# Case: the first W' tile from unsplit float32 pieces, stores issued by ScalarE, and earlier slots for w_out and w1/w2

## The chip, the cores and the metric

The kernel runs on one core of one Trainium2 chip. The metric is the time of one execution in microseconds on the device. Each engine works through its own list of instructions in order and waits for others through semaphores: PE (TensorE, matrix products), DVE (VectorE), ACT (ScalarE), POOL (GpSimd) and SP (SyncE, which here only issues DMAs).

## The reference

Three blocks follow each other, all in float32: attention with a decay by the running sum of `log f`, then two feed-forward blocks on the 2304 tokens of width 512.

```python
scores = scale * q @ k.T + cum[:, None] - cum[None, :]      # 4 x 8 heads, 576 x 576, causal
x = softmax(scores) @ v                                     # 2304 x 512
h = x @ w_in;  g = h * tanh(softplus(h));  x = g @ w_out    # 512 -> 2048 -> 512
h = (x @ w1) * (x @ w2) @ w3;  y = h @ w_out2               # 512 -> 1024 -> 1024 -> 512
```

## The kernel before

**Precision.** PE multiplies in a reduced float32 form ("fp32r" in the rows) at a high pace, so a product that must keep float32 accuracy is made of three: each operand is split into a rounded half `hi` and a rest `lo`, and hi·hi, hi·lo and lo·hi are added in PSUM (`MM_PAIRS`). A split is a cast by ACT (L98) and a subtraction by DVE (L102) or, in two pieces of 256 columns, by POOL (L112). Scores from raw q and k, the transposes and P·V use plain float32 operands.

**Weights.** The host passes them as 64-bit words. A piece of 128 x 512 is loaded (512 KB, L122) and converted by one ACT instruction (L133, `cv_exp`) and three DVE instructions (L141 to L143, `cv_bits`).

**Two phases.** Phase A (to about 380 us) works through 16 pairs of heads, four *sub-slots* (slots in the code) a pair, 64 in all and a few behind them. In a slot stand score products, softmax (minimum on DVE, L391; exponential on ACT, L401), transposes on PE (L438) with their copies out of PSUM by ACT and DVE (L453), and in every fourth slot P·V. Between them `run_filler` puts products of weights:

- Slots 0 to 20: W' = w3 @ w_out2, in eight tiles of 24 products (`wp_unit`, L521). Tile f needs two pieces of w3 (`t{f}0`, `t{f}1`) and all eight of w_out2 (`o0` to `o7`). The order of the tiles is `FS`: 0, 4, 1, 5 and so on. The ten pieces of the first tile are loaded, converted and split ahead of slot 0, with the subtractions on DVE (`lo_eng`); those of the later tiles are prepared in the slots, with POOL subtracting.
- From slot 21: the first layer x @ w_in (`l1_unit`, L552), 24 products a slot to slot 36, then 12. Each unit of 12 products is copied to a tile `h` (three buffers, L556) and stored to `h_scr` (L557).

Beside these, `job` gives pieces their slots: loading, conversion and what follows one slot later. w_out's pieces (`u`) start at `W_OUT_SLOT`; from pairs of them POOL forms sums and `build` (L837 to L850) writes seven split tiles a pair to DRAM through five rotating buffers (`pt`, `bs`). Four pieces of w1 and w2 (`v`) are converted and stored at slots 56 to 62. Phase B (from about 385 us) runs the feed-forward layers.

**Order.** PE's order is written out by hand. The other engines' orders come from a list scheduler that runs when the kernel is built; ahead of slot 0, ACT's, DVE's and SP's are by hand too. All DMAs are issued by SP. A DMA counts up one of eight semaphores in turn (`DMAHW0` to `DMAHW7` in the orders), and one that takes a semaphore again first waits for the DMA that had it eight DMAs before, unless another wait covers that.

`plan` (L589) spreads the 192 products of W' over slots 0 to 20 in the shares 26, 24, 22 and 24 of a pair's four slots. `R` (L420) is a pair's row of inverse sums, loaded from `inv_scr`, where `inv_rows` stored it; P·V's result is multiplied by it (L483).

Of the kernel before, what the change touches and what calls it, by code (L numbers as in the profile page):

```python
# [24 lines left out]
TB = S // 2  # L25
# [21 lines left out]
W_IN_SLOT = 16  # L47
L1_BOTH = 6
W_IN_STEP = 0.8
W_OUT_SLOT = 30  # L50
W_OUT_STEP = 1.8
V_SOON = 4
L1_S = (21, 37)
SHARE = (26, 24, 22, 24)

# [20 lines left out]
class Kernel:  # L76
# [48 lines left out]
    def cv_exp(self, key):  # L125
        raw = self.cv[key][0]
        if key in self.soon:
            t = self.x_tile(f"cv{key}", F32)[:, :512]
        else:
            t = self.att.tile([128, 512], F32, name=f"cv{key}", tag="cv", bufs=CV)  # L130
        self.cv[key][1] = t
        hw = raw.rearrange("p (n w) -> p n w", w=2)[:, :, 1]
        self.nc.scalar.activation(t, f32(hw), AF.Copy, scale=F64_EXP)  # L133

    def cv_bits(self, key):

# [275 lines left out]
    def inv_rows(self, p):  # L412

        nc = self.nc
        t = self.att.tile([16, 128], F32, name=f"inv{p}", tag="inv", bufs=1)
        with self.tc.high_priority(offset=HP_SM):
            nc.scalar.copy(t[0:9], self.ps_t[1][0:9, 384:512])
        nc.sync.dma_start(self.inv_scr[p], t[0:9])

    def inv_load(self, p):  # L420
        self.R = self.att.tile([128, S], F32, name=f"R{p}", tag="R", bufs=1)
# [80 lines left out]
    def w3_split(self, f, k):  # L502
# [2 lines left out]
        hi, lo = self.w3s[f]  # L505
        self.cv_split(f"t{f}{k}", hi[:, 512 * k:512 * k + 512], lo[:, 512 * k:512 * k + 512])

    def wp_unit(self, f):

        mm = self.nc.tensor.matmul  # L510
        steps = []
        box = []

        def step(g, k, i):
            if i == 0:
                box.append(self.l1_bank())
            o = box[0]
            a, b = MM_PAIRS[k]
            w = self.w3s[f][a][:, 128 * g:128 * g + 128]
            x = self.wo2t[g][:, 512 * b:512 * b + 512]  # L520
            mm(o, w, x, start=i == 0, stop=i == 23)  # L521
            if i == 23:
                t = self.w_tile(0, f"wp{f}", F32)[:, :512]
                with self.tc.high_priority(offset=HP_L1):
                    self.nc.scalar.copy(t, o)
                self.nc.sync.dma_start(self.wp_scr[f], t)

        i = 0
        for g in range(8):
            for k in range(3):  # L530
                steps.append(((f"t{f}{g // 4}", f"o{g}"), lambda g=g, k=k, i=i: step(g, k, i)))
                i += 1
        return steps
# [6 lines left out]
    def l1_unit(self, b, m, half):  # L540
        mm = self.nc.tensor.matmul
        steps = []
        box = []

        def step(c, k, i):
            if i == 0:
                box.append(self.l1_bank())
            o = box[0]
            a, bb = MM_PAIRS[k]
            w = self.wi[m][:, 512 * a + 128 * c:512 * a + 128 * c + 128]  # L550
            x = self.X[4 * b + c, half][:, TB * bb:TB * bb + TB]
            mm(o[:, :TB], w, x, start=i == 0, stop=i == 11)  # L552
            if i == 11:
                t = self.base.tile([128, TB], F32, name=f"h{b}_{m}_{half}", tag="h", bufs=HB)
                with self.tc.high_priority(offset=HP_L1):
                    self.nc.scalar.copy(t, o[:, :TB])  # L556
                self.nc.sync.dma_start(self.h_scr[128 * m:128 * m + 128, b * S + TB * half:b * S + TB * half + TB], t)  # L557

        i = 0
        for c in range(4):  # L560
            for k in range(3):
                steps.append(((f"i{m}",), lambda c=c, k=k, i=i: step(c, k, i)))
                i += 1
        return steps
# [23 lines left out]

    def plan(self):  # L589

        cnt, acc, done = [], 0.0, 0
        share = [SHARE[s % NU] for s in range(WP_END)]
        for x in share:
            acc += 192 * x / sum(share)
            k = min(192, int(acc + 0.5)) - done
            cnt.append(k)
            done += k
        cnt += [24] * (L1_S[1] - WP_END) + [12] * 22 + [0] * (NU * NPAIR - L1_S[1] - 22)
# [2 lines left out]
    def phase_a(self):  # L601
# [5 lines left out]

        first = []
        for q in range(2):
            first.append((f"t0{q}", self.cols(self.w3t, 0, q), self.w3_split, 0, q))  # L610
            for g in range(4 * q, 4 * q + 4):
                first.append((f"o{g}", self.rows(self.wo2, g), self.wo2_split, g))
        where = [None, None, 8, 8, 8, 8, 0, 0, 0, 0]
        def early(a, z):
            for i in range(a, z):
                self.cv_load(first[i][0], first[i][1], where[i])

        def go(i):
            self.cv_exp(first[i][0])
            self.last = self.cv_bits(first[i][0])  # L620

        def fin(i):
            first[i][2](*first[i][3:])

        self.consts()
        self.lo_eng = "dve"
        with self.tc.manual_schedule(engines={getattr(mybir.EngineType, e) for e in ("Activation", "DVE", "SP")}):
# [6 lines left out]
            for i in range(1, len(first)):  # L634
                go(i)
                if i == HOLD:
                    self.hold = self.last
                fin(i - 1)
            fin(9)
        self.lo_eng = "pool"  # L640
        self.go_act, self.go_sp = self.last_act, self.last_sp

# [7 lines left out]
        def job(s, key, src, fin, *a, lag=1):  # L650
            at(max(0, s - 1), self.cv_load, key, src)
            conv.setdefault(s + lag, []).append(key)
            at(s + lag + 1, fin, *a)

        jobs = [(f"t{f}{q}", self.cols(self.w3t, f, q), self.w3_split, f, q) for f in FS[1:] for q in range(2)]
        for i, j in enumerate(jobs):
            job(int(W3_STEP * i), *j)
# [9 lines left out]
                for k in range(2):  # L667
                    at(s + 4 + k, self.build, 0, u, k)
        for f in range(V_SOON):
            job(NU * NPAIR - 8 + 2 * f, f"v{f}", self.v_src(f), self.cv_store, f"v{f}", self.w12_scr[f])  # L670
        at(32, self.x_places, 1)
        for p in range(4, 8):
            for half, s in ((0, (32, 33, 34, 36)), (1, (38, 38, 39, 40))):
# [8 lines left out]
                for hh in range(2):  # L682
                    at(s + 1, self.load_cum, 2 * p + 2 + hh)

        for f in FS:
            self.filler.extend(self.wp_unit(f))
        self.S, self.nsm, self.act, self.dve = {}, 0, None, None
        with self.tc.manual_schedule(engines={mybir.EngineType.PE}):
# [647 lines left out]
```

## Time and profile before

| | |
|---|---|
| median of 3 runs | 930.57 us (929.39 to 933.74) |
| profiled execution | 932.73 us, span 930.8 us |
| PE busy | 876.7 us, 94% of the span |
| DVE, ACT, POOL busy | 688.4, 499.0, 147.4 us |
| DMA queue of SP | 189.0 MB, 63.7% of 16 engines' span |

The profiled execution lies 2.2 us above the median, and 1.9 us of it lie around the span. A matmul's busy time is modelled and overlaps the next; two starts in a row give the pace. Durations below are of this execution.

### The profile page before, as it was taken

The numbers are of one execution on the slowest core, as the hardware profiler recorded it, in microseconds if no ns is written. First come the engines' busy times: TensorE is split into PE (matmuls) and PEld (weight loads), VectorE is DVE, ScalarE is ACT, GpSimd is POOL, SyncE is SP. The second block draws the span as 40 slices with busy tenths as digits, with TensorE's granted clock in tenths as the row PEclk, the third lists the DMA queues.
The fourth block names the chain that finished last, engine by engine and source line by source line (L and its number), as shares of the span: only waits on it lengthen the run. The fifth ranks groups of instructions, "written<-read, shape, count | busy, mean of one in ns | idle before, by whom it ended". The sixth has DMA issues, their size and how long they took to land.

```text
span 930.8 us, 17585 instructions
## 1 busy us (share of the span) xinstructions
PE 876.7 (94%) x6338; PEld 807.0 (87%) x6338; DVE 688.4 (74%) x1361; ACT 499.0 (54%) x1091; POOL 147.4 (16%) x197
## 2 busy tenths in 40 slices
PE   2699999999999888899999999999999999999998
PEld 1477778888877657899999999999999999999998
DVE  8977796645756566978897989789778887544483
ACT  2756666556755655656654556455585444322152
POOL 4043443314655442000000000000000000000000
PEclk9899999999999989999999999999999999999999
DMA  6965566757687874324565548998997555555552
GB/s 191 262 180 180 166 199 205 217 149 225 217 248 245 246 257 164 104 72 146 157 226 171 178 155 303 345 338 290 412 320 205 156 163 161 166 171 159 166 176 77
DMA packets 129190, 190.11 MB, mean 204 GB/s; under 512 B 12352, under 2 KB 70736, under 8 KB 129104
## 3 DMA queue, kind: packets, MB, share of 16 engines
q1 hardware_dynamic: 129104, 189.00, 63.7%
q8 instruction: 50, 0.82, 0.4%
q14 instruction: 36, 0.29, 0.1%
HBM read 131.44 MB, written 57.52 MB: 203 GB/s over the span
## 4 chain that ended last, share of the span: by engine, by line
PE 63%; DMA 8%; ACT 4%; DVE 3%; issue 3%; POOL 2%; SPq 1%; ACTq 0%; POOLq 0%; DVEq 0%
PE ps_x L993 15%; PE ps_x L1065 14%; PE ps_z L1065 7%; PE ps_y L993 6%; PE ps_z L993 6%; PE ps_l L552 5%; PE ps_y L1065 3%; DMA ws<-ws 2%; PE ps_s L371 2%; DMA ws<-pt 1%; DMA cvru<-in_w_out_dram 1%; PE ps_s L472 1%; PE ps_t L438 1%; POOL pt L849 1%; DMA ws<-bs 1%
## 5 line engine op out<-in xcount | busy, mean ns | idle before, releaser
L552 PE MATMUL ps_l<-x,wi 128*128 128x288 f32 x696 | 102.3, 300 | 3.0 <-ACT h L556 3.0
L552 PEld LDWEIGHTS ps_l<-x,wi 128*128 128x128 f32 x696 | 94.1, 189 | 8.4 <-issue 3.5
L954 ACT CAST g_h<-y 128x576 fp32r<-128x576 f32 x96 | 63.7, 675 | 55.0 <-PE ps_x L993 26.0
L993 PE MATMUL ps_x<-g_h,ws 128*128 128x288 f32 x512 | 91.5, 296 | 1.2 <-ACT g_h L954 1.0
L955 DVE TENSOR_TENSOR g_l<-y,g_h 128x576 fp32r<-128x576 f32 x96 | 72.4, 755 | 16.0 <-ACT g_h L954 14.4
L401 ACT ACTIVATE P<-P,sum 128x256 f32<-128x256 f32 (+3 forms) x112 | 70.5, 632 | 21.7 <-DVE sum L391 16.1
L993 PEld LDWEIGHTS ps_x<-g_h,ws 128*128 128x128 f32 x512 | 75.8, 189 | 2.1 <-ACT g_h L954 1.5
L391 DVE CUSTOM_DVE_ANT_0 P<-ps_s,m 128x256 f32<-128x256 f32 (+2 forms) x96 | 48.4, 553 | 19.4 <-PE ps_s L371 19.4
L453 DVE COPY pt<-ps_t 128x128 f32<-128x128 f32 (+1 forms) x64 | 29.8, 486 | 42.2 <-PE ps_t L438 41.6
L993 PE MATMUL ps_x<-g_l,ws 128*128 128x288 f32 x256 | 55.2, 296 | 0.5 <-DVE g_l L955 0.5
L371 PE MATMUL ps_s<-raw 64*128 64x128 f32 (+3 forms) x256 | 49.1, 499 | 6.8 <-DMA raw<-in_qk_dram 5.6
L1065 PE MATMUL ps_x<-T,gs 128*128 128x288 f32 x384 | 54.1, 296 | 0.9 <-ACT Cg L1070 0.9
L1065 PE MATMUL ps_x<-T,ws 128*128 128x288 f32 x384 | 53.8, 295 | 0.0
L1065 PEld LDWEIGHTS ps_x<-T,gs 128*128 128x128 f32 x384 | 52.0, 188 | 1.1 <-ACT Cg L1070 1.1
L1065 PEld LDWEIGHTS ps_x<-T,ws 128*128 128x128 f32 x384 | 51.9, 188 | 0.0
L521 PE MATMUL ps_l<-wo,w3h 128*128 128x512 f32 x128 | 46.2, 431 | 5.5 <-DVE wo L102 4.0
L954 ACT CAST h_h<-ab 128x576 fp32r<-128x576 f32 x48 | 31.7, 673 | 34.2 <-PE ps_x L993 20.1
L993 PE MATMUL ps_x<-h_h,ws 128*128 128x288 f32 x256 | 46.3, 297 | 1.6 <-DMA ws<-ws 1.5
L955 DVE TENSOR_TENSOR h_l<-ab,h_h 128x576 fp32r<-128x576 f32 x48 | 36.0, 755 | 15.7 <-ACT h_h L954 15.6
L472 PE MATMUL ps_s<-pt,va 128*64 128x320 f32 (+3 forms) x384 | 45.0, 383 | 0.0
L438 PE MATMUL ps_t<-ident,P 128*128 128x128 f32 x288 | 40.5, 278 | 2.7 <-ACT pt L453 2.7
L993 PEld LDWEIGHTS ps_x<-g_l,ws 128*128 128x128 f32 x256 | 41.1, 189 | 1.0 <-DVE g_l L955 1.0
(278 smaller groups left out, 2181.9 us busy)
## 6 DMA issues: line engine op xcount, KB each, us to landing
ws<-ws SPq DMA_DIRECT2D x112, 512.0 KB
ws<-gs SPq DMA_DIRECT2D x84, 256.0 KB
ws<-pt SPq DMA_DIRECT2D x45, 256.0 KB
h_scr<-h SPq DMA_DIRECT2D x64, 144.0 KB
y<-h_scr SPq DMA_DIRECT2D x16, 576.0 KB
cvrt<-in_w3t_dram SPq DMA_DIRECT2D x16, 512.0 KB
cvri<-in_w_in_dram SPq DMA_DIRECT2D x16, 512.0 KB
cvru<-in_w_out_dram SPq DMA_DIRECT2D x16, 512.0 KB
```

What stands on the lines that cost most here:

```text
L371: mm(ps[:, 512 * hh:512 * hh + n], t[r, q0:q0 + 128], t[r, 0:n], start=first, stop=not first)
L391: dve = ttr(P[hh][:, :n], ps[:, 512 * hh:512 * hh + n], self.m1[:, 512 - n:], -0.125, 3.0e38, ALU.add, ALU.min, st[hh])
L401: ins = nc.scalar.activation(t[:, :n], t[:, :n], AF.Exp, bias=b, scale=-1.0, accum_out=self.sums[:, i:i + 1])
L438: tr(self.ps_t[hh][:, o + 128 * k:o + 128 * k + 128], P[:, 128 * k:128 * k + 128], self.ident)
L453: return copy(dst[:, 0:c + 1, 128 * c:128 * c + 128], src)
L472: mm(ps[64 * hh:64 * hh + 64, 256 + q:256 + q + w], lhs, rhs, start=i == 0, stop=i == len(plan) - 1)
L521: mm(o, w, x, start=i == 0, stop=i == 23)
L552: mm(o[:, :TB], w, x, start=i == 0, stop=i == 11)
L954: self.mark(self.nc.scalar.copy(hi, raw))
L955: self.mark(self.nc.vector.tensor_tensor(lo, raw, f32(hi), ALU.subtract))
L993: mm(ps[:, r, :TB], w[:, 256 * a + 128 * e:256 * a + 128 * e + 128], ops[i][b][:, r], start=o in (1, 5, 2) and f == 0 and (a, b) == (0, 0) ...
L1065: mm(bank[:, r, :TB], w[:, i:i + 128], T[o, k][:, b, r], start=o in (1, 2, 5) and (k, a, b) == (0, 0, 0), stop=(k, a, b) == (1, 1, 0), ski ...
```

## The change

Four things change.

1. The first W' tile (f = 0) is made by `wp_raw`: eight products of unsplit float32 pieces, four in slot 0 and four in slot 1. `t00` and `t01` are not split any more. The eight pieces of w_out2 are converted ahead of slot 0 as before, but split in slots 1 to 3, where POOL subtracts. The 168 products of the seven other tiles are spread over slots 2 to 20.
2. The stores of W' tiles, of `inv` and of `h` (8, 16 and 64 DMAs) are issued by ACT, in ACT's order, and no longer by SP.
3. w_out's pieces start at slot 29 with a step of 1.7 slots (before: 30 and 1.8).
4. The four pieces of w1 and w2 are prepared at slots 33, 39, 45 and 51 (before: 56, 58, 60 and 62).

```diff
-W_OUT_SLOT = 30
-W_OUT_STEP = 1.8
+W_OUT_SLOT = 29
+W_OUT_STEP = 1.7
+V_SLOT = 33

...
-        nc.sync.dma_start(self.inv_scr[p], t[0:9])
+        nc.scalar.dma_start(self.inv_scr[p], t[0:9])

...
+    def wp_out(self, f, o):
+        t = self.w_tile(0, f"wp{f}", F32)[:, :512]
+        with self.tc.high_priority(offset=HP_L1):
+            self.nc.scalar.copy(t, o)
+        self.nc.scalar.dma_start(self.wp_scr[f], t)
+    def wp_raw(self, w, x):
+        box = []
+        def step(g):
+            if g == 0:
+                box.append(self.l1_bank())
+            self.nc.tensor.matmul(box[0], w[g // 4][:, 128 * (g % 4):128 * (g % 4) + 128], x[g],
+                                  start=g == 0, stop=g == 7)
+            if g == 7:
+                self.wp_out(0, box[0])
+        return [((), lambda g=g: step(g)) for g in range(8)]

...
-                t = self.w_tile(0, f"wp{f}", F32)[:, :512]
-                with self.tc.high_priority(offset=HP_L1):
-                    self.nc.scalar.copy(t, o)
-                self.nc.sync.dma_start(self.wp_scr[f], t)
+                self.wp_out(f, o)

...
-                self.nc.sync.dma_start(self.h_scr[128 * m:128 * m + 128, b * S + TB * half:b * S + TB * half + TB], t)
+                self.nc.scalar.dma_start(self.h_scr[128 * m:128 * m + 128, b * S + TB * half:b * S + TB * half + TB], t)

...
-        cnt, acc, done = [], 0.0, 0
-        share = [SHARE[s % NU] for s in range(WP_END)]
+        cnt, acc, done = [4, 4], 0.0, 0
+        share = [SHARE[s % NU] for s in range(2, WP_END)]
-            acc += 192 * x / sum(share)
-            k = min(192, int(acc + 0.5)) - done
+            acc += 168 * x / sum(share)
+            k = min(168, int(acc + 0.5)) - done

...
-                fin(i - 1)
-            fin(9)

...
+        raw = [[self.cv[key][1] for key in keys] for keys in (("t00", "t01"), [f"o{g}" for g in range(8)])]
+        self.filler.extend(self.wp_raw(*raw))
+        for g in range(8):
+            at(1 + g // 3, self.wo2_split, g)

...
-            job(NU * NPAIR - 8 + 2 * f, f"v{f}", self.v_src(f), self.cv_store, f"v{f}", self.w12_scr[f])
+            job(V_SLOT + 6 * f, f"v{f}", self.v_src(f), self.cv_store, f"v{f}", self.w12_scr[f])

...
-        for f in FS:
+        for f in FS[1:]:

```

How the orders move shows at three places. The first is PE around slot 2, before; `w3h_400` and `w3l_401` are the halves of tile 4's w3 pieces, `w3h_226` and `w3l_227` those of tile 0, `wo_g` the split pieces of w_out2.

```order
L374 MATMUL ps_s_79<-aug_95 128x288 x2
L521 MATMUL ps_l_83<-wo_6_290,w3h_226 128x512
L521 MATMUL ps_l_83<-wo_6_290,w3l_227 128x512
L521 MATMUL ps_l_83<-wo_7_293,w3h_226 128x512 x2
L521 MATMUL ps_l_83<-wo_7_293,w3l_227 128x512
L438 MATMUL ps_t_80<-ident,P_0_99 128x128 x3
L438 MATMUL ps_t_81<-ident,P_1_100 128x128 x3
L521 MATMUL ps_l_82<-wo_0_235,w3h_400 128x512 x2
L521 MATMUL ps_l_82<-wo_0_235,w3l_401 128x512
```

The same place after the change, from the last two unsplit products on (`cvo_256` and `cvo_261` are the unsplit `o6` and `o7`, `cvt_241` the unsplit `t01`; `w3h_382` and `w3l_383` are now the halves of tile 4).

```order
L523 MATMUL ps_l_83<-cvo_256,cvt_241 128x512
L523 MATMUL ps_l_83<-cvo_261,cvt_241 128x512
L439 MATMUL ps_t_80<-ident,pt 128x128
L439 MATMUL ps_t_81<-ident,pt 128x128
L439 MATMUL ps_t_80<-ident,P_0_97 128x128 x2
L439 MATMUL ps_t_81<-ident,P_1_98 128x128 x2
L375 MATMUL ps_s_79<-raw_93 128x288 x2
L375 MATMUL ps_s_79<-aug_95 128x288 x2
L439 MATMUL ps_t_80<-ident,P_0_99 128x128 x3
L439 MATMUL ps_t_81<-ident,P_1_100 128x128 x3
L543 MATMUL ps_l_82<-wo_0_324,w3h_382 128x512 x2
L543 MATMUL ps_l_82<-wo_0_324,w3l_383 128x512
```

No split product stands ahead of the transposes of `P_0_99` any more, and tile 4's first `w3l` product stands where it stood, behind them. The second place is POOL behind its last memory set, before and then after.

```order
L319 MEMSET aug_96 4x64
L112 TENSOR_TENSOR w3l_401<-cvt_337,w3h_400 128x256 x2
L112 TENSOR_TENSOR w3l_401<-cvt_384,w3h_400 128x256 x2
L112 TENSOR_TENSOR w3l_481<-cvt_419,w3h_480 128x256 x2
L112 TENSOR_TENSOR w3l_481<-cvt_453,w3h_480 128x256 x2
```

After the change POOL goes on there with the pieces of w_out2.

```order
L320 MEMSET aug_96 4x64
L113 TENSOR_TENSOR wo_0_324<-cvo_221,wo_0_324 128x256 x2
L113 TENSOR_TENSOR wo_1_328<-cvo_226,wo_1_328 128x256 x2
L113 TENSOR_TENSOR wo_2_332<-cvo_231,wo_2_332 128x256 x2
L113 TENSOR_TENSOR wo_3_370<-cvo_236,wo_3_370 128x256 x2
L113 TENSOR_TENSOR wo_4_374<-cvo_246,wo_4_374 128x256 x2
L113 TENSOR_TENSOR wo_5_378<-cvo_251,wo_5_378 128x256 x2
L113 TENSOR_TENSOR w3l_383<-cvt_301,w3h_382 128x256 x2
L113 TENSOR_TENSOR wo_6_414<-cvo_256,wo_6_414 128x256 x2
L113 TENSOR_TENSOR wo_7_418<-cvo_261,wo_7_418 128x256 x2
L113 TENSOR_TENSOR w3l_383<-cvt_358,w3h_382 128x256 x2
```

Tile 4's first `w3l` was POOL's first subtraction and is now its seventh. The casts that feed these stand on ACT, after the change, as follows (`cvt_439` is a piece of tile 1 whose load is waited for, `P_0_103` the last softmax of the pair).

```order
L99 CAST wo_2_332<-cvo_231 128x512
L134 ACTIVATE cvt_397<-cvrt_336 128x512
L134 ACTIVATE cvt_439<-cvrt_387 128x512
L513 COPY wp_345<-ps_l_83 128x512
L454 COPY pt<-ps_t_80 128x128
L454 COPY pt<-ps_t_80 128x2x128
L514 DMA wp_scr<-wp_345 128x512
L454 COPY pt<-ps_t_80 128x3x128
L402 ACTIVATE P_0_103,sum_277<-P_0_103,sum_277 128x576
L99 CAST wo_3_370<-cvo_236 128x512
L99 CAST wo_4_374<-cvo_246 128x512
L99 CAST wo_5_378<-cvo_251 128x512
```

`wo_3`'s cast and those after it stand behind the wait for a load, the copies of the transposes and an exponential. The third place is ACT where `h` is copied out in slot 32, before, with what each row waits for (buffer numbers kept).

```order
L401 ACTIVATE P3_0_101,sum8_2086<-P3_0_101,sum8_2086 128x512 [waits DVE_49]
L556 COPY h0_8_1_2188<-ps_l1_83 128x288 [waits DMAHW6_49,PE_49,Activation_49]
L401 ACTIVATE P3_1_102,sum8_2086<-P3_1_102,sum8_2086 128x512 [waits DVE_49]
L98 CAST x5_0_2116<-xr5_1764 128x288
L556 COPY h0_9_1_2213<-ps_l0_82 128x288 [waits DMAHW7_49,PE_49,Activation_49]
L453 COPY pt_88<-ps_t0_80 128x128 [waits PE_49]
L453 COPY pt_88<-ps_t0_80 128x2x128
```

The same rows of ACT after the change hold the stores too.

```order
L402 ACTIVATE P3_0_101,sum8_2079<-P3_0_101,sum8_2079 128x512 [waits DVE_49]
L575 COPY h0_8_1_2176<-ps_l1_83 128x288 [waits DMAHW7_49,PE_49]
L402 ACTIVATE P3_1_102,sum8_2079<-P3_1_102,sum8_2079 128x512 [waits DVE_49]
L99 CAST x5_0_2109<-xr5_1750 128x288
L576 DMA h_scr_61<-h0_8_1_2176 128x288 [waits DMAHW1_49,Activation_49]
L575 COPY h0_9_1_2207<-ps_l0_82 128x288 [waits DMAHW0_49,PE_49]
L454 COPY pt_88<-ps_t0_80 128x128 [waits PE_49]
L454 COPY pt_88<-ps_t0_80 128x2x128
L576 DMA h_scr_61<-h0_9_1_2207 128x288 [waits DMAHW2_49,Activation_49]
```

A store of `h` now stands among ACT's copies and exponentials, and waits there for a DMA semaphore; 66 of the 88 stores that moved have such a wait. SP's list goes from 665 rows to 572.

## Rows read from the trace of the kernel before

**Rows 1.** The page's part 1: busy time, share of the span, instructions.
```profile
PE 876.7 (94%) x6338; PEld 807.0 (87%) x6338; DVE 688.4 (74%) x1361; ACT 499.0 (54%) x1091; POOL 147.4 (16%) x197
```

**Rows 2.** Busy time by stretch: stretch, length, engines, clock, DMA share, GB/s.
```profile
0.00:60.00 60.00, 34.35 (x139) 23.61 (x140) 51.02 (x122) 30.76 (x72) 15.51 (x39) 0.91 0.71 209
60.00:140.00 80.00, 80.00 (x514) 61.28 (x513) 64.73 (x162) 53.20 (x151) 33.11 (x38) 1.00 0.64 186
140.00:235.00 95.00, 91.97 (x707) 79.92 (x706) 54.84 (x146) 57.70 (x171) 32.39 (x39) 1.00 0.67 198
235.00:345.00 110.00, 98.70 (x734) 78.40 (x733) 69.46 (x189) 66.77 (x212) 56.38 (x70) 0.96 0.78 243
345.00:391.00 46.00, 40.35 (x279) 35.15 (x280) 36.68 (x85) 26.02 (x73) 10.03 (x11) 0.90 0.40 135
```

**Rows 3.** Timeline, 20 to 51 us: start, duration, what, [idle before and releaser].
```profile
20.41 0.67 ACT L133 ACTIVATE cvo<-cvro 128x512 f32<-128x512 f32 x1 [1.40 <-DMA cvro<-in_wo_dram]
23.36 0.68 ACT L133 ACTIVATE cvt<-cvrt 128x512 f32<-128x512 f32 x1 [1.77 <-DMA cvrt<-in_w3t_dram]
...
42.08 0.68 ACT L133 ACTIVATE cvt<-cvrt 128x512 f32<-128x512 f32 x1 [1.53 <-DMA cvrt<-in_w3t_dram]
...
43.23 0.88 PE L438 MATMUL ps_t<-ident,P 128*128 128x128 f32 x6 [1.73 <-ACT pt L453]
...
44.98 0.73 PE L521 MATMUL ps_l<-wo,w3h 128*128 128x512 f32 x2 [0.87 <-ACT w3h L98]
...
45.08 4.21 POOL L112 TENSOR_TENSOR w3l<-cvt,w3h 128x256 fp32r<-128x256 f32 x4 [33.96 <-ACT w3h L98]
...
46.35 0.50 PE L521 MATMUL ps_l<-wo,w3l 128*128 128x512 f32 x1 [0.64 <-POOL w3l L112]
...
50.33 1.03 PE L438 MATMUL ps_t<-ident,P 128*128 128x128 f32 x8
```

**Rows 4.** Groups by line over the span: shapes, count, busy and mean ns.
```profile
L112 POOL TENSOR_TENSOR w3l<-cvt,w3h 128x256 fp32r<-128x256 f32 x28 | 24.7, 906 | 64.9 <-ACT w3h L98 53.1 <-issue 10.1 <-PE ps_t L442 1.5
L102 DVE TENSOR_TENSOR wo<-cvo,wo 128x512 fp32r<-128x512 f32 x8 | 5.5, 686 | 0.1
L98 ACT CAST wo<-cvo 128x512 fp32r<-128x512 f32 x8 | 4.9, 612 | 4.7 <-DVE cvo L143 4.7
```

**Rows 5.** Timeline of POOL and PE, 55 to 63 us.
```profile
55.13 1.49 POOL L112 TENSOR_TENSOR w3l<-cvt,w3h 128x256 fp32r<-128x256 f32 x2 [5.84 <-ACT w3h L98]
...
60.48 1.14 PE L374 MATMUL ps_s<-raw 128*128 128x288 f32 x4
61.24 0.64 PE L374 MATMUL ps_s<-aug 128*128 128x288 f32 x2
...
62.18 0.62 PE L521 MATMUL ps_l<-wo,w3h 128*128 128x512 f32 x2
62.64 0.39 PE L521 MATMUL ps_l<-wo,w3l 128*128 128x512 f32 x1
```

**Rows 6.** Waits, 235 to 372 us (PE) and 240 to 340 us (ACT): total, times, longest.
```profile
PE ps_t L442 <- ACT pt L453: 7.7, 4, 3.9
...
ACT pt L848 <- DMA ws<-pt: 18.6, 8, 6.6
```

**Rows 7.** SP's stores of `h`, and one copy with its store.
```profile
L557 SPq DMA_DIRECT2D h_scr<-h x64: 319/360/1822, 140.0 to 379.2; - x64
...
275.43 0.39 ACT L556 COPY h<-ps_l 128x288 f32<-128x288 f32 x1
...
280.25 0.56 SPq L557 DMA_DIRECT2D h_scr<-h  x1
```

**Rows 8.** Timeline of PE: first score products of a sub-slot, twice.
```profile
74.78 1.77 PE L371 MATMUL ps_s<-raw 64*128 64x384 f32 x8
...
326.06 2.85 PE L371 MATMUL ps_s<-raw 64*128 64x384 f32 x8
```

More of the change, by code (lines that the diff above doesn't have):

```diff
@@ L132, in cv_exp @@
         hw = raw.rearrange("p (n w) -> p n w", w=2)[:, :, 1]
-        self.nc.scalar.activation(t, f32(hw), AF.Copy, scale=F64_EXP)
+        return self.nc.scalar.activation(t, f32(hw), AF.Copy, scale=F64_EXP)
     def cv_bits(self, key):
@@ L609, in phase_a @@
         for q in range(2):
-            first.append((f"t0{q}", self.cols(self.w3t, 0, q), self.w3_split, 0, q))
+            first.append((f"t0{q}", self.cols(self.w3t, 0, q)))
             for g in range(4 * q, 4 * q + 4):
-                first.append((f"o{g}", self.rows(self.wo2, g), self.wo2_split, g))
+                first.append((f"o{g}", self.rows(self.wo2, g)))
         where = [None, None, 8, 8, 8, 8, 0, 0, 0, 0]
@@ L618, in go @@
         def go(i):
-            self.cv_exp(first[i][0])
+            self.last_act = self.cv_exp(first[i][0])
             self.last = self.cv_bits(first[i][0])
-        def fin(i):
-            first[i][2](*first[i][3:])
         self.consts()
```

## The prediction, made before the run

> **What bounds the kernel now.** I read the page's busy shares first, then the table by stretch, then waits and timelines of the stretches that the change touches. PE is busy 94% of the span [rows 1], so what matters is when PE stands still, and at which clock it runs. The table by stretch [rows 2] shows where that is. Up to 60 us PE does 34.4 us of work, and the clock is 0.91. From 60 to 140 us it has no gap: 80.0 of 80.0, while DVE, ACT and POOL are at 81%, 67% and 41%. In 140 to 235 us it lacks 3.0 us, in 235 to 345 us 11.3 us at a clock of 0.96, in 345 to 391 us 5.7 us. So a delay that arises before 60 us is carried through to 140 us in full, since nothing but PE is late there, and it can only be made good where PE waits, in some 20 us of gaps behind 140 us.
>
> **The start: parts removed and moved.** The change takes ten subtractions of 686 ns, 6.9 us, from DVE ahead of slot 2 [rows 4], and 24 split products from PE. The reader is to see in [rows 3] why little of this arrives. ACT stands still for loads at 20.41 us (o3), at 23.36 us (t01) and at 42.08 us (the second piece of tile 1). The loads ahead of them are the same as before, in the same order, and the DMA engines are busy 0.71 of this stretch on average [rows 2]; I take these landings as fixed. Behind the last of them, in the order before and after, stand ACT's copies of the transposes, and PE waits for these at 43.23 us. So PE's transposes of slot 2 cannot come earlier by more than a fraction of a microsecond: I count the 6.9 us of DVE as nothing, because the loads cover them. If that cover is thinner than I think, up to 1.7 us, PE's wait at 43.23 us, is gained.
>
> Then the price. PE next needs tile 4's first w3l product. Before, it ran at 46.35 us, 1.27 us behind the start of POOL's first subtraction at 45.08 us [rows 3]. Now it waits for POOL's seventh piece, and wo_3 is cast only after the load of 42.08 us. Before, 2.9 us lay between that landing and the product that waited for the cast of w3h (42.08 to 44.98 us): a conversion, two copies of transposes, an exponential, PE's next transposes, their copy and the cast. Now the same steps end with wo_3's cast, with two more in the row: the copy of the first W' tile, as large as the cast of 612 ns [rows 4], 0.6 us; and the exponential of P_0_103, which stood beside PE's transposes and now stands behind their copy, 0.6 us (PE's transposes took 0.88 us in the row of 43.23 us). That makes 46.1 us; the store of the W' tile, 0.4 us, takes the exponential's place beside the transposes. POOL then does wo_3, wo_4, wo_5 and half of a w3l piece, 7 instructions at 906 ns [rows 4]: 6.3 us, so 52.4 us. The casts of the later pieces follow at 0.6 us each and are ready in time. POOL's two bounds are 0.75 us an instruction [rows 5] (51.3 us) and 1.05 us, the four in 4.21 us of [rows 3] (53.4 us). Against 46.35 us that is 6.0 us late (5.0 to 7.0). Behind this product the same ten or so products stand on PE before the transposes that came at 50.33 us, so these move by as much. What else is there is hidden: wo_6, wo_7 and the second half of tile 4 take five pieces' time on POOL while PE does its twelve products, scores and transposes; and the number of products still to do is about equal (146 before, 144 now, as the two orders show at the scores that follow).
>
> The Trainium skill bears on this split. The measured row has a subtraction of 128 x 512 at 686 ns on DVE and, in two halves, at 1812 ns on POOL [rows 4]. Its page "GPSIMD Engine Reference", section "Engine selection", advises against such work on GpSimd, which it puts at about twice as slow for operations with two inputs. The trace agrees in direction and is worse, 2.6 times; by the page's factor the seven halves would take 4.8 us and the delay would be 4.5 us and the time 931 us.
>
> The eight unsplit products are not shown before at this width. One plain float32 product is two instructions; for 288 columns four of them took 0.76 us (60.48 to 61.24 us), 0.38 us a product, against 0.23 us for a split product of 512 columns (62.18 to 62.64 us, two of them) [rows 5]. By width a plain product of 512 columns takes 0.68 us, eight 5.4 us; the 24 that go took 5.5 us. The lower bound is two passes at 0.23 us, 3.7 us in all, the upper one the doubled 0.68 us at the lower clock, 10.9 us. I take 5.4 us and nothing for the difference: the last four wait for conversions anyway, and they end some 3 us ahead of the copies that PE waits for. At the upper bound these 3 us cover the 2.7 us that four products lose.
>
> **Stores from ACT.** 88 stores leave SP. A store of h takes SP 360 ns in the median, 319 to 1822 ns [rows 7], and it comes late: the copy of 275.43 us is stored at 280.25 us. In 235 to 345 us some 22 of the 64 and five of inv stand in SP's list; at 0.45 us, between the median and the 0.56 us of that row, they take 12 us of 110. SP's lateness reaches PE through the five staging buffers: ACT waits 18.6 us for stores from them, PE 7.7 us for ACT's copies behind that [rows 6]. On the one side SP gets 12 us back and gives 3 us of it for the denser w_out and the earlier w1/w2. On the other side ACT, busy 66.8 of 110 us [rows 2], takes the 12 us over. It also waits in three stores of four for the DMA that stands eight places ahead, which SP has to issue and which has to land first; where SP is 4 to 5 us behind, as at 280.25 us, that is a wait of 2 to 4 us, and what queues behind it are the copies and exponentials that PE needs.
>
> **W_out and w1/w2 earlier.** 320 to 350 us holds PE's longest gap, 3.9 us [rows 6], and the lower clock behind it: eight score instructions took 2.85 us there instead of 1.77 us [rows 8]. The four pieces, 0.75 MB each of loads and stores by their shapes, leave it, which should return about 4 us; the same 3 MB go to stretches at a DMA share of 0.67 and 0.78 [rows 2] and cost perhaps 1 us.
>
> For 140 to 391 us I bound the sum from above by all gaps, 20 us, and the lower clock, 0.04 of 110 us and 0.10 of 46 us, 9 us, and from below by ACT's 12 us and an equal amount of waits, of which half reaches PE, -12 us. I take a gain of 4 us, near the one term with a row of its own, the gap at 325 us.
>
> **Sum.** 932.7 + 6.0 - 4 = 934.7 us on the profiled execution's scale. That execution lies 2.2 us above the median, so on the scale of the runs 932.5 us; I say 933.
>
> **Rivals.** *ACT becomes the late engine* (slower). Place: 235 to 345 us, ACT's stores among its copies. Some 17 stores wait for a semaphore; at 1 us each that is 17 us of ACT beside 12 us of issuing, and of its 43 us without work there 18.6 us are already waits for the staging buffers [rows 6]. If half reaches PE, 235 to 345 us grows by 10 us or more and the start's 6 us stay: 938 to 946 us. It decides from about 0.5 us a store on. Against it: SP, relieved, is less late.
>
> *SP's relief dominates* (faster). SP's stores of staging buffers come 2 to 4 us earlier, ACT's 18.6 us shrink to a few, and PE's gaps of 11.3 us and the lower clock behind them go, and 3 us of the tail: -16 us, and +6 of the start: 915 to 925 us. For it speaks that SP is 4.4 us behind at 280 us [rows 7]; against it that SP loses only 93 of its 665 rows in all.
>
> *Nothing saved by another queue.* The store of 280.25 us was late because of SP's list [rows 7], not because of the engines. The Trainium skill's "DMA: Bandwidth & Descriptors", section "Issuing engines are not separate DMA queues", says that a second issuing engine saves only the sequencer's issuing time, usually small, since all DMAs share the same 16 engines. By it, if the 0.78 share of 235 to 345 us [rows 2] is what binds, the gaps stay as they are and only the start counts: 936.5 us on the runs' scale, just above the forecast's own range.
>
> *The start is not late*: the load of 42.08 us lands earlier, wo_3 is cast by 41 us and POOL is through by 47 us: 926 to 928 us.
>
> **Chances.** Forecast, 928 to 936 us: 0.32. Nothing saved by another queue: 0.09. ACT late: 0.29. SP's relief: 0.24. Start not late: 0.06. A measurement of this kernel can tell about 0.5%, 4.7 us, from no change. Faster (under 925.9 us): 0.23 of relief, 0.03 of the start, 0.01 of the forecast, 0.27. Slower (over 935.2 us): 0.28 of ACT, 0.06 of the other queue, 0.02 of the forecast, 0.36. Same: the rest of each, 0.37. The range of 8 in 10 is 921 to 945 us; the forecast's own is 928 to 936 us.
>
> **What would show it.** Right: PE's first w3l product of the second tile at 51 to 54 us, with POOL as its releaser, and the transposes behind it 5 to 7 us later than 50.33 us; PE without gaps from about 62 to 145 us; a stretch from slot 21 to the end of phase A shorter by 2 to 6 us; ACT's waits for DMA at the new stores short in sum. Wrong: that product under 49 us; ACT waiting over 10 us in sum at its stores; PE's gaps between 235 and 345 us down to under 3 us.

## The result and the profile after

The changed kernel takes 940.83 us in the median of six runs (937.35 to 946.89), the kernel before 930.17 us; the ratio is 1.0108, 95% interval 1.0079 to 1.0137. It is slower by 1.1%. A second set gave 942.95 us and 1.0103 (1.0079 to 1.0127).

The profiled execution is the fastest of the first six: 937.35 us, span 935.4 us, against 932.73 and 930.8 us. Part 1 of its page answers to [rows 1]; the table by stretch (columns as there) to [rows 2], with one stretch more at the end.

```profile
PE 879.5 (94%) x6330; PEld 806.7 (86%) x6330; DVE 680.4 (73%) x1351; ACT 499.1 (53%) x1089; POOL 157.9 (17%) x213
```

```profile
0.00:60.00 60.00, 30.04 (x95) 17.89 (x96) 40.05 (x96) 24.61 (x53) 25.26 (x53) 0.86 0.68 200
60.00:140.00 80.00, 80.00 (x501) 59.98 (x501) 63.12 (x161) 53.22 (x153) 33.51 (x38) 1.00 0.58 179
140.00:235.00 95.00, 94.37 (x726) 82.13 (x724) 60.69 (x157) 59.90 (x173) 34.80 (x42) 1.00 0.70 213
235.00:345.00 110.00, 100.80 (x728) 80.72 (x726) 72.80 (x195) 71.71 (x228) 61.25 (x77) 0.95 0.80 253
345.00:391.00 46.00, 43.02 (x336) 37.93 (x333) 32.72 (x82) 24.54 (x68) 3.05 (x5) 1.00 0.31 103
391.00:410.00 19.00, 15.29 (x104) 15.02 (x103) 11.54 (x23) 10.04 (x14) 0.00 (x0) 0.91 0.21 67
```

PE does 4.3 us less before 60 us, has no gap to 140 us, and does more than before in each of the next three stretches. Then comes a stretch in which before had no gap at all (19.0 of 19.0 us at full clock): here 3.7 us are missing and the clock is 0.91.

The start, in PE's timeline and then POOL's (start, duration, what, [idle before and releaser]), answers to [rows 3]:

```profile
21.74 6.51 PE L523 MATMUL ps_l<-cvo,cvt 128*128 128x512 f32 x8
...
36.44 1.12 PE L523 MATMUL ps_l<-cvo,cvt 128*128 128x512 f32 x2 [3.31 <-DVE cvo L144]
...
43.50 0.88 PE L439 MATMUL ps_t<-ident,P 128*128 128x128 f32 x6 [2.49 <-ACT pt L454]
47.45 1.22 PE L543 MATMUL ps_l<-wo,w3h 128*128 128x512 f32 x2 [3.07 <-ACT w3h L99]
52.15 0.79 PE L543 MATMUL ps_l<-wo,w3l 128*128 128x512 f32 x1 [3.48 <-POOL w3l L113]
...
56.58 1.81 PE L439 MATMUL ps_t<-ident,P 128*128 128x128 f32 x8
```

```profile
45.91 5.50 POOL L113 TENSOR_TENSOR wo<-cvo,wo 128x256 fp32r<-128x256 f32 x6 [4.90 <-DVE cvt L143]
51.37 1.41 POOL L113 TENSOR_TENSOR w3l<-cvt,w3h 128x256 fp32r<-128x256 f32 x2
```

The first w3l product waits for POOL and runs at 52.15 us instead of 46.35 us; the transposes behind it start at 56.58 us instead of 50.33 us. The first P·V (its last rows) starts at 74.89 us instead of 67.17 us.

The end of the story is at 392 us, in PE's timeline and then ACT's:

```profile
390.25 1.75 PE L1083 MATMUL ps_x<-TX,wi 128*128 128x288 f32 x12
395.71 3.01 PE L1083 MATMUL ps_z<-TX,sp 128*128 128x288 f32 x12 [3.71 <-ACT sp L1152]
398.53 2.20 PE L1083 MATMUL ps_x<-TX,wi 128*128 128x288 f32 x12
```

```profile
392.04 0.64 ACT L1088 COPY Cx<-ps_x 128x576 f32<-128x576 f32 x1 [4.76 <-PE ps_x L1083]
392.70 1.28 ACT L1177 ACT_TABLE_LOAD   x1
393.99 1.16 ACT L1177 ACTIVATE y<-Cx 128x1152 f32<-128x1152 f32 x1
395.06 1.12 ACT L1152 CAST sp<-sr 128x512 fp32r<-128x512 f32 x2
```

PE waits for `sp`, the sums of w_in's pieces for the second output tile. Their cast stands behind a copy, a table load and the Mish activation. In the order before, the first cast stood ahead of all three, as ACT's timeline of the kernel before shows:

```profile
391.56 0.62 ACT L1134 CAST sp<-sr 128x512 fp32r<-128x512 f32 x1 [2.78 <-DVE sr L1125]
392.20 1.28 ACT L1159 ACT_TABLE_LOAD   x1
393.50 1.17 ACT L1159 ACTIVATE y<-Cx 128x1152 f32<-128x1152 f32 x1
394.57 0.61 ACT L1134 CAST sp<-sr 128x512 fp32r<-128x512 f32 x1
395.08 0.63 ACT L1070 COPY Cx<-ps_x 128x576 f32<-128x576 f32 x1
```

On DVE the sums stood ahead of two additions to `Cx`. No line of the diff is near: the scheduler's lists came out otherwise here because what stands ahead of them changed. With the first tile's change alone the order stays as before, so it is the stores or the slots that turn it; which of these is not shown.

### The profile page after: what moved, and what is told of

It reads as the page before. It is cut to its first block, busy times and chain, and to the rows that moved or that the text cites. A ratio compares the mean times of both kernels' runs of the same rounds, so it can differ in the third digit from the quotient of the medians.

```text
span 935.4 us, 17550 instructions
## 1 busy us (share of the span) xinstructions
PE 879.5 (94%) x6330; PEld 806.7 (86%) x6330; DVE 680.4 (73%) x1351; ACT 499.1 (53%) x1089; POOL 157.9 (17%) x213
## 4 chain that ended last, share of the span: by engine, by line
PE 59%; DMA 4%; DVE 2%; ACT 2%; issue 1%; ACTq 0%; SPq 0%; DVEq 0%
PE ps_x L1083 15%; PE ps_x L1011 14%; PE ps_z L1083 8%; PE ps_z L1011 6%; PE ps_y L1011 6%; PE ps_y L1083 4%; DMA ws<-ws 3%; PE ps_l L571 2%; PE ps_s L473 1%; PE ps_s L372 1%; PE ps_t L439 1%; DMA ws<-pt 1%; PE ps_s L375 1%; PE ps_x L571 1%; DVE g_l L973 0%
## 5 line engine op out<-in xcount | busy, mean ns | idle before, releaser
L973 DVE TENSOR_TENSOR g_l<-y,g_h 128x576 fp32r<-128x576 f32 x96 | 72.3, 754 | 16.0 <-ACT g_h L972 14.3
L1083 PEld LDWEIGHTS ps_x<-T,ws 128*128 128x128 f32 x384 | 52.1, 188 | 0.0
L372 PE MATMUL ps_s<-raw 64*128 64x128 f32 (+3 forms) x256 | 46.1, 474 | 5.7 <-DMA raw<-in_qk_dram 5.6
L439 PEld LDWEIGHTS ps_t<-ident,P 128*128 128x128 f32 x288 | 34.8, 145 | 8.6 <-ACT pt L454 6.8
```

The source lines that it names most:

```text
L372: mm(ps[:, 512 * hh:512 * hh + n], t[r, q0:q0 + 128], t[r, 0:n], start=first, stop=not first)
L439: tr(self.ps_t[hh][:, o + 128 * k:o + 128 * k + 128], P[:, 128 * k:128 * k + 128], self.ident)
L973: self.mark(self.nc.vector.tensor_tensor(lo, raw, f32(hi), ALU.subtract))
L1083: mm(bank[:, r, :TB], w[:, i:i + 128], T[o, k][:, b, r], start=o in (1, 2, 5) and (k, a, b) == (0, 0, 0), stop=(k, a, b) == (1, 1, 0), ski ...
```

## The experiments

The table cuts the profiled executions at three places of PE's timeline: the last rows of the first P·V, those of the ninth (both from the groups `ps_s<-pt,vb`), and the first product of x @ w_in on `ps_x`. Columns: when the first is reached, the time from mark to mark, and from the last mark to the end of the span; then the timed runs. Ratios are against the kernel before, with their intervals.

| kernel | first P·V | to ninth | to x·w_in | to end | median us | ratio |
|---|---|---|---|---|---|---|
| before | 67.2 | 172.7 | 129.1 | 561.9 | 930.17 | |
| changed | 74.9 | 169.6 | 124.4 | 566.5 | 940.83 | 1.0108 |
| changed, second time | 75.6 | 170.5 | 129.7 | 565.6 | 942.95 | 1.0103 (1.0079-1.0127) |
| changed, order put back | 73.6 | 170.1 | 130.0 | 561.9 | 938.00 | 1.0061 (1.0039-1.0084) |
| first tile alone | 75.0 | 173.3 | 128.1 | 564.6 | 942.67 | 1.0102 (1.0079-1.0124) |
| stores + slots | 65.7 | 169.6 | 127.4 | 563.8 | 933.51 | 1.0009 (0.9984-1.0033) |
| stores + slots, order | 65.9 | 173.0 | 130.3 | 561.4 | 930.61 | 0.9994 (0.9973-1.0015) |
| the same, w1/w2 late | 65.4 | 171.1 | 122.8 | 561.5 | 923.72 | 0.9909 (0.9877-0.9940) |
| the same, w1/w2 early, own buffers | 66.5 | 170.8 | 126.6 | 563.3 | 927.92 | 0.9951 (0.9929-0.9974) |
| stores, order | 65.9 | 170.0 | 125.1 | 562.6 | 929.63 | 0.9990 (0.9969-1.0012) |
| w_out's slots, order | 64.6 | 172.6 | 126.5 | 562.3 | 927.85 | 0.9954 (0.9934-0.9975) |
| changed, DVE subtracts | 70.2 | 170.0 | 130.1 | 566.9 | 938.26 | 1.0057 (1.0035-1.0080) |
| changed, w1/w2 late | 75.4 | 169.8 | 123.4 | 566.3 | 936.97 | 1.0055 (1.0030-1.0080) |
| changed, all three repairs | 71.5 | 171.3 | 121.2 | 561.9 | 927.38 | 0.9941 (0.9920-0.9962) |

"Order" means that the order of before at 390 us is put back by hand; in "first tile alone" it stayed by itself. The rows come from different chips, and a profile is one of 6 to 12 runs that spread over 5 to 12 us: the stretches tell where, the ratios how much.

**The changed kernel again.** 

> The changed kernel once more, for a second profile and a narrower ratio. The first profiled execution (937.35 us) stands at the low end of its six runs (937 to 947 us) and is 4.6 us above before: 7.7 us late at the first P.V, no longer late at 369 us, late again from a 3.7 us gap of PE at 392 us on. Theory: the start and the 392 us gap are there in every execution, and what differs between executions is how much of the 7.7 us is made good between 140 and 369 us; a slower execution then reaches the first x @ w_in product on ps_x (368.9 us before) 3 to 9 us later. Rival: the slower executions lose it in phase B, behind 400 us, and reach that product at the same 369 us. Median 938 to 943 us by either.

The x·w_in product came at 375.75 us, 6.8 us later than in the first profile, and the tail was about as long as there. So the theory holds: of the 6.8 us, 5.3 us arise between the ninth P·V and x·w_in (129.7 us against 124.4 us). PE's gaps of 235 to 366 us are 9.2 us in five pieces in the first execution and 14.1 us in nine here, nearly all behind ACT's copies of the transposes; why they fall differently is not settled.

What both executions share is a wait of ACT. In 235 to 350 us of the second, the view of waits (total, times, longest) has

```profile
ACT cvu L134 <- DMA w_scr<-cvv: 10.4, 3, 6.7
```

and the longest of these three is, in the timelines of SP, ACT and PE,

```profile
291.89 0.32 SPq L151 DMA_DIRECT2D w_scr<-cvv  x1
```

```profile
296.05 0.67 ACT L134 ACTIVATE cvu<-cvru 128x512 f32<-128x512 f32 x1 [6.67 <-DMA w_scr<-cvv]
...
300.04 0.25 ACT L456 COPY pt<-ps_t 64x128 f32<-64x128 f32 x1
```

```profile
300.34 0.33 PE L439 MATMUL ps_t<-ident,pt 128*128 128x128 f32 x1 [2.23 <-ACT pt L456]
```

The four buffers `cv` are shared by all converted pieces. A piece of w_out is used up on the chip, by POOL's sums and ACT's casts; one of w1 or w2 keeps its buffer until its store has landed. ACT's conversion that needs this buffer stands still for that, and the exponentials and the transposes' copy behind it reach PE late. In the first profile SP issues the store at 288.77 us, and the same conversion waits under another name:

```profile
292.73 0.67 ACT L134 ACTIVATE cvu<-cvru 128x512 f32<-128x512 f32 x1 [5.35 <-DMA h_scr<-h]
```

A releaser is inferred; the place in the list and the 4 us from the store's issue to the conversion, the same in both, say that it is the same wait.

**The order at 390 us put back** (lists of DVE and ACT only):

```diff
+        self.s2 = add(s2, s1, a11, ALU.subtract)
...
-            if o == 1:
-                self.mark(nc.scalar.copy(d[:, 0], ps))
+                with self.behind(self.sp0 if (name, m) == ("x", 1) else None):
+                    self.mark(nc.scalar.copy(d[:, 0], ps))
```

On DVE two additions to `Cx` are put behind `s2` in the same way.

> The changed kernel, with the order of ACT and DVE at the start of phase B (around 390 us) put back to that of before: the sums and the first cast of the second output tile's weights stand ahead of the copy and the Mish activation again. Theory (the 3.7 us gap of PE at 392 us and the lower clock behind it come from that order alone): 4 to 5 us faster than the changed kernel, 935 to 937 us, and no gap over 1 us there. Rival (the late operand is late because of what comes before, so the gap moves elsewhere): within 1.5 us of the changed kernel.

938.0 us, just above the 935 to 937 us expected, a ratio of 1.0061 against 1.0103 on the same chip. In the timeline the gap of 3.71 us is gone, with two small ones left, and the clock stays up:

```profile
394.97 1.76 PE L1083 MATMUL ps_x<-TX,wi 128*128 128x288 f32 x12
397.05 0.76 PE L1083 MATMUL ps_z<-TX,sp 128*128 128x288 f32 x4 [0.33 <-DVE Cx L1098]
398.56 1.32 PE L1083 MATMUL ps_z<-TX,sp 128*128 128x288 f32 x8 [0.75 <-DVE sp L1156]
```

The tails of the table go the same way: 561.4 to 563.3 us where that order was put back, 563.8 to 566.9 us where the stores are ACT's and it was not.

**The first tile's change alone.** The diff without ACT's stores and without the new slots. 

> The kernel before with only the first tile's change: unsplit products for W' tile 0, w_out2's pieces split in slots 1 to 3 on POOL. Stores stay with SP, w_out and w1/w2 keep their slots. Theory (this part costs the start, the others pay it back): 7 to 8 us late at the first P.V as in the changed kernel; 20 us of PE's gaps between 140 and 391 us can take up part of it; 933 to 938 us. Rival (the start's delay is taken up by the gaps whatever the stores do): 929 to 932 us. Rival (ACT's stores make the loss, not this part): below 931 us, with the first P.V late all the same.

942.67 us: this part alone costs as much as the whole change, and none of the three expected ranges held it. The gaps of 140 to 369 us took up nothing (172.7 + 129.1 us before, 173.3 + 128.1 here). 2.7 us more go in the tail. 1.6 us of them arise by 400 us, where PE restarts at a lower clock behind its gap:

```profile
376.34 2.06 PE L571 MATMUL ps_x<-x,wi 128*128 128x288 f32 x12 [3.23 <-DVE xr L484]
378.20 3.08 PE L571 MATMUL ps_y<-x,wi 128*128 128x288 f32 x12
...
393.79 2.44 PE L1083 MATMUL ps_x<-TX,sp 128*128 128x288 f32 x12 [2.99 <-ACT Cx L1088]
```

The kernel before has the second gap too (2.98 us at 384.86 us), and behind the first one it restarts at the higher pace:

```profile
368.91 1.86 PE L552 MATMUL ps_x<-x,wi 128*128 128x288 f32 x12 [2.67 <-DVE xr L483]
370.61 1.75 PE L552 MATMUL ps_y<-x,wi 128*128 128x288 f32 x12
```

**The two other parts alone.** The diff without the first tile's change. 

> The kernel before with the two other parts: the stores of W', inv and h from ACT, and the earlier slots of w_out and w1/w2; the first tile as before. Theory (these gain in 140 to 369 us and lose 4 to 5 us at 392 us by the new order): first P.V at 67.2 us as before, the product of 368.9 us 3 to 7 us earlier, total 926 to 931 us. Rival (ACT is the late engine): that product later than before, total 934 us or more. Rival (the gaps of before took up the late start anyway and the two parts gain nothing): product within 1 us of 368.9 us, total 933 to 936 us.

933.51 us, no measurable change, between the theory and the rival of no gain. The profiled execution was the fastest of twelve and showed a product 6.3 us early; that is one execution and not the kernel. **With the order put back:** 

> The kernel with the stores from ACT and the earlier slots, the first tile as before, and the order of ACT and DVE around 390 us put back as in the run on the changed kernel. Theory (that order costs 4 to 5 us wherever it appears, and the run without it showed it at the same place): 4 us faster than the same kernel without the repair (933.5 us), so 927 to 931 us, some 3 us faster than before. Rival (there is nothing to gain there, since the y activation delayed by it is needed later): 932 to 935 us.

930.61 us. The tail fell from 563.8 to 561.4 us, but the ratios' intervals overlap: 0.9994 against 1.0009 is not resolved.

**w1/w2 late again.**

```diff
-            job(33 + 6 * f, f"v{f}", ...
+            job(NU * NPAIR - 8 + 2 * f, f"v{f}", ...
```

> As the kernel with stores, slots and repaired order, but the four pieces of w1 and w2 back at slots 56 to 62. Theory (in the w_out stretch each of these pieces holds a conversion buffer until its store has landed, and ACT's next conversion of w_out waits 2.5 to 6.7 us for it, 10 us in three waits; PE's gaps of 240 to 320 us come from that): those waits are gone, PE's gaps between 235 and 320 us shrink by 3 to 5 us, and a gap of 2 to 4 us comes back at 320 to 350 us: within 2 us of that kernel. Rival (the move is the part that gained, by emptying 320 to 350 us): 3 to 5 us slower than it. Rival (the waits for the buffers cost more than they save): 3 us or more faster than it.

923.72 us, 0.9909: the second rival, that the waits cost more than they save. The move of four pieces cost 0.85% (0.9994 to 0.9909), in the profiles 7.5 us in the stretch to x·w_in (130.3 against 122.8 us). The gap that was to come back stands at 327.00 us (2.64 us, behind ACT's copy), but PE's gaps of 235 to 320 us fell from 9.6 us to 5.8 us. Busy times by stretch:

```profile
235.00:345.00 110.00, 101.19 (x741) 79.84 (x738) 72.93 (x200) 73.44 (x235) 60.82 (x77) 0.97 0.83 263
345.00:391.00 46.00, 43.14 (x327) 40.81 (x324) 34.57 (x77) 25.76 (x55) 0.00 (x0) 0.96 0.26 89
```

**w1/w2 early, in buffers of their own.**

```diff
-        if key in self.soon:
+        if key in self.soon or key[0] == "v":
             t = self.x_tile(f"cv{key}", F32)[:, :512]
```

> As the kernel with stores, slots and repaired order (930.6 us), the pieces of w1 and w2 still at slots 33 to 51, but converted into buffers of another ring, which nothing of w_out uses at that time. Theory (what the earlier w1/w2 pieces cost is ACT's conversion of w_out waiting for a buffer until their store has landed, 10.4 us in three waits): these waits are gone, PE's gaps of 240 to 325 us shrink from 13 us to 8 or less, and the time falls most of the way to the 923.7 us of the kernel with late pieces: 922 to 926 us. Rival (they cost by their place in the lists of SP, DVE and ACT or by their 3 MB of traffic): still 929 us or more.

927.92 us, 0.9951: about half of the way, above the range expected, and the intervals of 0.9951 and 0.9994 touch. ACT's waits for the stores are gone. So the shared buffers are about half of the cost by the medians, but how that reaches PE is not shown: PE's gaps of 240 to 325 us did not shrink to 8 us, they are 14.3 us against 12.9 us with shared buffers. What fell from the ninth P·V to x·w_in is PE's busy time for the same work, 111.3 us at a clock of 0.99 against 115.5 us at 0.95. Whether the other half is their place in the lists, their traffic, or waits for the other ring stays open.

**The changed kernel with w1/w2 late.** 

> The changed kernel with the four pieces of w1 and w2 back at slots 56 to 62, all else as changed. Theory (the move costs the same 7 us here as in the kernel without the first tile's change): 934 to 937 us. Rival (in the changed kernel all is later by the start, so the wait for these stores hits a gap that is there anyway): 939 us or more.

936.97 us, 1.0055 against 1.0103: 4.5 us, on the theory's side.

**The stores alone.** 

> The kernel before with only the stores of W', inv and h moved to ACT, and the order around 390 us put back. Theory (SP's relief gains 3 to 5 us in 140 to 235 us, where PE waited for the copies of h, and little behind it): 927 to 930 us. Rival (ACT pays for the issuing): 933 us or more. Rival (the slots' shift made all of the gain): 931 to 933 us.

929.63 us, 0.9990: no measurable gain, though the profiled execution, the fastest of twelve, gained 7 us. **w_out's slots alone:** 

> The kernel before with only w_out's slots moved (29 and 1.7) and the order around 390 us kept; stores with SP, w1/w2 late. Beside it stand the stores with order, 929.6 us, and stores with w_out's slots, 923.7 us. Theory (the denser w_out needs SP's relief: with the stores in SP's list it is late there): 930 to 934 us, no gain. Rival (w_out's slots gain their 6 us alone): 925 to 927 us.

927.85 us, 0.9954: better than the theory, short of the rival. With the stores beside it, it was 0.9909. So the denser w_out gains without SP's relief. Beside it the stores seem to gain a further 0.45%; the intervals (0.9934 to 0.9975 and 0.9877 to 0.9940) overlap a little, so this is not shown. The traces point the same way: in 235 to 350 us ACT waits 24.9 us for stores of the staging buffers `pt` with SP issuing, 17.7 us with ACT issuing. By themselves the stores agree with the Trainium skill, "DMA: Bandwidth & Descriptors", section "Issuing engines are not separate DMA queues": another issuing engine saves only the sequencer's time.

**w_out2 subtracted on DVE.**

```diff
+        self.lo_eng = "dve"
         self.cv_split(f"o{g}", t[:, :512], t[:, 512:])
+        self.lo_eng = "pool"
```

> The changed kernel, but w_out2's pieces are subtracted on DVE (690 ns each) in slots 1 to 3 instead of on POOL (1.8 us each). Theory (the start is late because tile 4's first w3l stands behind seven half pieces on POOL): the first w3l product comes at 47.5 to 49.5 us instead of 52.15 us, bounded by ACT's cast of w3h at 47.45 us; the first P.V at 70 to 72 us instead of 75; 936 to 939 us, 3 to 5 us faster than the changed kernel. Rival (DVE's 5.5 us of subtractions delay the softmax instead, since DVE is 80% busy there): first P.V at 74 us or later, 941 us or more.

938.26 us, as expected. The first w3l product came at 49.01 us, now behind ACT's cast:

```profile
47.99 1.22 PE L545 MATMUL ps_l<-wo,w3h 128*128 128x512 f32 x2 [3.07 <-ACT w3h L99]
49.01 0.69 PE L545 MATMUL ps_l<-wo,w3l 128*128 128x512 f32 x1
```

**All three repairs.** DVE subtracts, w1/w2 late, order put back. 

> The changed kernel with three repairs at once: w_out2's pieces subtracted on DVE, the pieces of w1 and w2 late, the order around 390 us put back. It differs from the 923.7 us kernel only by the unsplit first tile. Theory (the rest of the start's loss stays: tile 4's w3h cast stands on ACT behind six others, 47 us instead of 45): 3 to 5 us above that kernel, 926 to 929 us. Rival (the start's loss is taken up by gaps): within 1.5 us of it.

927.38 us, 3.7 us above the kernel without the unsplit tile, as the theory had it, though the intervals of the two ratios overlap (0.9920 to 0.9962 and 0.9877 to 0.9940). The best of all is then the kernel before with the stores on ACT, w_out at slot 29 with step 1.7, w1/w2 late and the order kept: 923.72 us, faster than both kernels.

## Why the prediction was right or wrong

The sign of the sum and the range of 8 in 10 (921 to 945 us) held, the size did not: 933 us was forecast, 940.83 us came, 8 us more, outside the forecast's own 928 to 936 us. It lies where the rival of the late ACT had it (938 to 946 us), whose mechanism showed only in small part. The start was understood; behind 140 us the gain of 4 us did not come and a cost came that no term had, so that the wide range held is in part luck.

- **The start: right, a little short.** "7 instructions at 906 ns … 6.3 us, so 52.4 us": POOL's six took 5.50 us and the seventh ended near 52.1 us; the product ran at 52.15 us. Predicted were +6.0 us (5.0 to 7.0); +5.8 us came at the product, +6.25 us at the transposes, +7.7 us at the first P·V. Of the 1.5 us between the last two, 0.8 us is the clock, 0.86 instead of 0.91 up to 60 us: the eight transposes took 1.81 us instead of 1.03 us. The other 0.7 us is three more split products (0.23 us each) that now stand ahead of the first P·V. In the timed runs the part costs 9.5 us (1.0102), with 2.7 us of the profile's loss behind 376 us, which the prediction had not looked at.
- **What makes tile 4 late: POOL, and a cast.** How much of it is POOL is shown by DVE: 3.1 of the 5.8 us at the product, about 5 us at the first P·V. The other 2.7 us are a term that the prediction did not have, by the releaser of PE's row: ACT casts tile 4's w3h behind three pieces of w_out2, at 46.78 us instead of 44.31 us, and with DVE subtracting PE waits for that cast. All sixteen halves of w_out2 took POOL 0.83 us in the mean (0.92 us the six shown), 1.65 us a piece; DVE took 0.69 us a piece ahead of slot 0 and 0.89 us in slots 1 to 3. That is 2.4 and 1.9 times, where the prediction had 2.6 from w3's pieces. The Trainium skill's "GPSIMD Engine Reference", section "Engine selection", says about twice, and these runs agree.
- **The eight unsplit products: the upper bound.** They took 6.51 + 2.84 + 1.12 us, 10.5 us, near the bound of 10.9 us and not the 5.4 us taken (11.0 us in the run of the first tile alone, above the bound). It was hidden, as argued: the last product, two instructions, waited 3.3 us for a conversion, and the transposes that wait for ACT's copies came at 43.50 us instead of 43.23 us.
- **"ACT takes the 12 us over … a wait of 2 to 4 us": mostly wrong.** The group of ACT's stores of h (count, shortest, median and longest ns):

```profile
L576 ACTq DMA_DIRECT2D h_scr<-h x64: 325/327/562, 144.8 to 379.5; - x64
L576 ACTq EVENT_SEMAPHORE  x45: 17/17/17, 143.6 to 365.1; - x45
```

  The 64 issues take 21.7 us in sum. Laid beside ACT's timeline, 13.5 us of that run beside its own work, as in these three rows of the second execution, and 8.2 us fall where ACT runs nothing:

```profile
252.82 0.59 ACT L454 COPY pt<-ps_t 128x512 f32<-128x512 f32 x1
252.96 0.33 ACTq L576 DMA_DIRECT2D h_scr<-h  x1
253.33 0.69 ACT L134 ACTIVATE cvv<-cvrv 128x512 f32<-128x512 f32 x1
```

  The wait that was foretold exists. Its longest case in the second execution is a store for which ACT stands still until a load issued by SP has landed:

```profile
198.27 0.39 ACT L575 COPY h<-ps_l 128x288 f32<-128x288 f32 x1
200.99 0.33 ACTq L576 DMA_DIRECT2D h_scr<-h  x1
201.42 0.40 ACT L575 COPY h<-ps_l 128x288 f32<-128x288 f32 x1 [2.76 <-DMA cvrv<-in_w_dram]
```

  But it is rare. ACT stands idle ahead of the 64 stores for 6.0 us in sum in the first execution and 7.8 us in the second, 1.9 and 2.3 us at the longest; of that 2.2 and 2.6 us lie in 235 to 345 us, where the rival had 17 us. Nor did SP's relief do what the other rival had: ACT's waits for the staging buffers' stores went from 18.6 us to 14.7 us (17.7 us in the second execution). The stretch to the ninth P·V is shorter by about 2 to 3 us in most profiles with ACT's stores (169.6 to 171.3 us against 172.6 to 173.3; one at 173.0).
- **"The four pieces … which should return about 4 us … cost perhaps 1 us": the step that failed.** The gap at 325 us did go (the same transposes come at 334.15 us, without a wait), but it is also gone with the pieces back at their late slots (330.78 us in "changed, w1/w2 late"), so it was not theirs to return. The move had a net cost: 0.5% in the changed kernel (1.0103 against 1.0055) and 0.85% without the first tile's change. The earlier pieces hold buffers that w_out's conversions need, and ACT waits 9 to 13 us for these; by the run with buffers of their own that is about half of the cost. The prediction counted traffic and gaps and not who else uses the four buffers.
- **Missing from the sum: the order at 390 us.** 3.9 us by the timed runs (1.0103 against 1.0061), in a stretch where before had no gap and which was not read.
- **"Nothing saved by another queue"** held for the stores alone (0.9990); beside a denser w_out they may have saved something (0.9954 to 0.9909, not resolved).

From the ratios the parts add up, with 932 us for before: +9.5 for the first tile, -8.5 for stores and w_out's slots, +4.5 for w1/w2, +3.9 for the order: 9.4 us against the 9.6 and 10.1 us measured. Each part is uncertain by 2 us or more, and without the first tile's change w1/w2 cost more (0.85%) and the order less (0.15%, not resolved), so the close agreement is partly chance. Forecast were +6 for the first tile and -4 for all the rest, which by itself came to nothing (1.0009).

## What to carry to other kernels

Before moving a producer earlier, list everything that shares its ring of buffers and how long each holds one: a piece that is only stored holds its buffer until the store has landed, and the wait shows up on whoever takes that buffer next. Where a scheduler writes the lists, compare them to the end of the program and not only around the diff. When a stretch before an engine without gaps gets longer, count it in full, and take work off the slower engine first.

## What the runs showed of the hardware

DMAs issued by ACT cost the kernel nothing that could be measured: 13.5 of the 21.7 us of 64 issues lay beside ACT's running instructions, ACT stood idle 6.0 us in sum ahead of them, and the stores alone changed the time by a factor of 0.9990 (0.9969 to 1.0012). Plain float32 products of 512 columns took 0.95 us each in one stretch (2.84 us for three, at 30.29 us) and 1.63 us each in another (6.51 us for four, at 21.74 us, not long behind a 9.1 us wait of PE); the profile gives a granted clock of 1.00 in both, so it does not show why. And one kernel's executions spread over up to 12 us, so that profiles of a fastest run (stores alone, stores with slots) showed a gain that the median did not have.
